# A fused retention and gated-convolution kernel: 128x128 products turn keys and queries one double chunk ahead, the tensor engine's phase is cut in four, and keys arrive in float32

## The chip, the cores and the metric

The kernel runs on one core of a Trainium2 chip. The core has a tensor engine (PE in the profile, with PEld for its weight loads), a vector engine (DVE), a scalar engine (ACT), GpSimd (POOL) and a sync engine (SP) that here only issues transfers; 16 DMA engines move data between HBM and the on-chip memory SBUF. Matmul results land in a second memory, PSUM, in banks. The metric is the device time of one execution in microseconds; the median of three runs is given. The profile describes one execution, whose "span" is the time from its first to its last instruction.

## What is computed

Eight batches, eight heads, 576 tokens, head width 64. First a retention layer (attention with an exponential decay in place of the softmax), then a gated unit whose gate is a causal convolution over five tokens:

```python
scores = scale * np.matmul(q, k.transpose(0, 1, 3, 2))
gamma = 1.0 - 2.0 ** (-5.0 - np.arange(H))
Dmat = np.where(rel >= 0, gamma[:, None, None] ** rel[None], 0.0)   # rel = query position - key position
x = np.matmul(scores * Dmat, v)                 # then heads side by side: B x S x 512
gate_pre[:, t] = sum over k of conv_w[k] * x[:, t - 4 + k]           # 5 taps, zeros before the start
out = (sigmoid(gate_pre) * (x @ w_val)) @ w_out
```

All inputs and the output are float32: q, k and v are 9.4 MB each and so is the output, and the two weight matrices are 1 MB each.

## The kernel before

**Tiling.** 256 tokens of one batch (all eight heads) make a "double chunk". There are 18, numbered m: two for each of the eight batches, and after each group of four batches one "tail" that gathers the last 64 tokens of those four. Within a double chunk, token 2p+r sits on partition p, so that two tokens follow one another in a row; `ab` is the half of the partitions (the first or second 128 tokens), `pr` a pair of heads, `i` the head within it, `r` the token within its row. The decay is split into a factor by key token (`gin`, multiplied into the values) and one by query token (`gout`, multiplied into the result), so that in between only a 0/1 mask is needed.

**Steps for one double chunk m.** (1) Load q, k, v. (2) Cast to bfloat16: `cast_q`, and `cast_v` that also multiplies by `gin`, mostly on GpSimd. Keys, except the first ones, are loaded by `load_keys` (line 100): a DMA issued by GpSimd that casts on its way. (3) "Turn" keys and queries, so that the head width lies on the partitions: products with an identity matrix on the tensor engine into the PSUM bank `tps`, and a copy from there into `kq`. (4) `scores` (64x64 products of turned keys and queries), `masks` on the vector engine. (5) `update`: the state of the batch, keys times values, accumulated in the PSUM bank `st` and copied by `take_state` on the scalar engine. (6) `values` and `carried`: masked scores times values, plus state times queries, into the banks `o0` and `o1`; `take_x` (line 343) multiplies by `gout` on the vector engine and writes the result into the tile `xg`. (7) One double chunk later, `conv(m-1)`: 40 products of 64x64 with diagonal matrices, over shifted columns of `xg`, into two banks of the pool `psg`, and `gate` (a sigmoid on the scalar engine). (8) `value(m-1, i)`: eight products of 128x128 with `wvb`, and on the vector engine z = gate times value. (9) Two later, `project(m-2, i)`: four products of 128x128 with `wob`, copied by the scalar engine (line 433) and stored.

**Quarters and whole array.** Products with 64 rows and 64 columns use a quarter of the array, and four of them on different quarters run beside one another ("64*64" in the profile); `value` and `project` use the whole ("128*128").

**Order.** It is written out by hand: every engine takes its instructions in the order of the program. The tiling framework sets the waits between engines, by semaphores, from the tiles that instructions share. Start-up (lines 471 to 576) treats the first double chunks one by one, turns double chunks 1 to 4, and leaves the loop with two turned ahead. In the loop from line 578 one pass does, on the tensor engine: carried, scores, turning of half of m+2 mixed with `update(m, 1)`, convolution, values, carried, turning of the other half mixed with `update(m+1, 0)`, the end of the convolution, `scores(m+1, 0)` (all quarters), and then value, project, value, project (whole array). Turning a double chunk takes 64 products of 64x64 (line 268): 2 for keys and queries, 2 halves, 4 pairs, 2 tokens, 2 heads. `take_turned` (line 278) copies one half of keys and queries at once.

**Transfers.** Loads of q and v and the stores are issued by SP, in the program's order; q and v have five buffers (`LB = 5`), the bfloat16 keys seven.

Of the kernel before, what the change touches and what calls it, by code (L numbers as in the profile page):

```python
# [21 lines left out]
def kernel(  # L22
# [10 lines left out]
    nc = tc.nc  # L33
# [12 lines left out]
    LB = 5  # L46
# [33 lines left out]
    with tc.manual_schedule():  # L80
# [14 lines left out]
        def load(name, m):  # L95
            t = ld.tile([P, H, R, D], F32, name=f"f{name}", bufs=1 if name == "k" else LB)
            fetch(nc.sync, t, {"q": q, "k": k, "v": v}[name], m)
            loaded[name, m] = t

        def load_keys(m):  # L100

            kb = bfp.tile([P, H, R, D], BF16, name="kb", bufs=7)
            fetch(nc.gpsimd, kb, k, m)
            kbf[m] = kb

        cwn = consts.tile([KC * NP, P], F32, name="cwn")
        nc.scalar.dma_start(out=cwn, in_=moe_conv_w.rearrange("k (o i) -> (k o) i", i=P))
        load("k", 0)
        load("q", 0)
        load("v", 0)  # L110
        load("q", 1)
        load("v", 1)
# [9 lines left out]
        load_wv(nc.sync, 0)  # L122
        for m in range(2, LB + 1):
            load("q", m)
            load("v", m)
# [19 lines left out]
        load_keys(1)  # L145
# [44 lines left out]
        for pr in range(NP):  # L190
            nc.scalar.activation(gout[:, pr, :], posi, AF.Exp, bias=lsc, scale=lcol[:, pr:pr + 1])

        warm = consts.tile([P, 1], F32, name="warm")
        nc.scalar.activation(warm, lsc, AF.Sigmoid)
# [7 lines left out]
        tbank = ps_t.tile([P, 2, NP, R, HP], BF16, name="tps")  # L202
        whole = lambda t: t.rearrange("p a o r n -> p (a o r n)").bitcast(F32)
# [4 lines left out]
        def prep_conv_weights():  # L208
            cps = whole(tbank)[:, 0:KC * NP]
            nc.tensor.transpose(cps, cwn, identf[0:KC * NP, 0:KC * NP])  # L210
            cps = cps.rearrange("p (k o) -> p k o", k=KC)
            nc.vector.tensor_copy(cw[:, :, 0::2], cps[:, :, 0::2])
            for i in range(2):
                nc.vector.tensor_copy(cw[half[1 - i], :, 1::2], cps[half[i], :, 1::2])
# [11 lines left out]
        def cast(dst, src, copies):  # L226

            h = 0
            for (copy, n) in copies:
                copy(dst[:, h:h + n], src[:, h:h + n])  # L230
                h += n
            assert h == H

        def cast_k(m, *copies):
            kbf[m] = bfp.tile([P, H, R, D], BF16, name="kb", bufs=7)
            cast(kbf[m], loaded["k", m], copies)

        def cast_q(m, *copies):
            qbf[m] = bfp.tile([P, H, R, D], BF16, name="qb")
            cast(qbf[m], loaded["q", m], copies or ((nc.gpsimd.tensor_copy, H),))  # L240

        def cast_v(m, *engs):
            vbf[m] = bfp.tile([P, H, R, D], BF16, name="vb")
# [19 lines left out]
        def turns(which, m, ab, bank=None):  # L263

            src = (kbf, qbf)[which][m]
            dst = tbank[:, which] if bank is None else bank
            rows = half[ab]
            return [[(lambda pr=pr, r=r, i=i: nc.tensor.transpose(  # L268
                dst[half[i], pr, r, :], src[rows, 2 * pr + i, r, :], idb[rows, :]))
                for r in range(R) for i in range(2)] for pr in range(NP)]  # L270

        def turned_tile(m):
            if m not in kq:
                kq[m] = tp_sb.tile([P, 2, NP, 2, R, HP], BF16, name="kq")
            return kq[m]

        def take_turned(m, ab):
            nc.scalar.copy(turned_tile(m)[:, :, :, ab], tbank)  # L278
# [7 lines left out]
        def scores(m, r):  # L286
# [3 lines left out]
            return [[mm(s[i][half[ab], pr, 0:n], lhsT=kq[m][half[i], 0, pr, ab, r, :],  # L290
                        rhs=kq[m][half[i], 1, pr, ab, cols(m, r), :].rearrange("p r n -> p (r n)"),
# [32 lines left out]
        def carried(m, turn):  # L324
# [4 lines left out]
            for g in range(2):  # L329
                group = []  # L330
                for r in range(R) if kind == "tail" else (0,):
                    for i in range(2):
# [4 lines left out]
                        for pr in (2 * g, 2 * g + 1):  # L337
                            group.append(add(m, ab, pr, i, cols(m, r), lhsT=before[key][half[i], pr, :],
                                             rhs=kq[m][half[i], 1, pr, ab, cols(m, r), :].rearrange("p r n -> p (r n)")))
# [17 lines left out]
        def update(m, ab):  # L357
# [5 lines left out]
            return [[mm(st[b][half[i], pr, :], lhsT=kbf[m][half[ab], 2 * pr + i, r, :],  # L363
# [24 lines left out]
        def conv(n):  # L388

            g = [ps_g.tile([P, 2, 2 * P], F32, name="g") for _ in range(2)]  # L390
# [16 lines left out]

        def spare(pool, name):
            return pool.tile([P, DM], F32, name=name)
# [35 lines left out]
        def keep_warm(n):  # L445

            for _ in range(n):
                nc.tensor.matmul(whole(tbank), zeros[:, 0:P], zeros, start=True, stop=True)

        def turn_early(which, m, copies):  # L450

            banks = [ps_g.tile([P, NP, R, HP], BF16, name="g") for _ in range(2)]
            run(*[turns(which, m, ab, banks[ab]) for ab in range(2)])
            dst = turned_tile(m)[:, which]
            for ab in range(2):
                copies[ab](dst[:, :, ab], banks[ab])

        def turn_both(which, m, copies):

            src = (kbf, qbf)[which][m]  # L460
            bank = tbank.rearrange("p a o r n -> p (a o r n)").rearrange("p (o r n) -> p o r n", o=NP, r=R)
            for pr in range(NP):
                for r in range(R):
                    for i in range(2):
                        nc.tensor.transpose(bank[half[i], pr, r, :], src[:, 2 * pr + i, r, :], ident)  # L465
            dst = turned_tile(m)[:, which]
            for ab in range(2):
                copies[ab](dst[:, :, ab], bank[:, :, :, half[ab]])
# [3 lines left out]
        cast_k(0, (v_copy, 4), (s_copy, 4))  # L472
        turn_early(0, 0, (v_copy, s_copy))
        prep_conv_weights()
        keep_warm(5)
        cast_q(0, (v_copy, 4), (s_copy, 4))
        turn_early(1, 0, (v_copy, s_copy))
        load_wv(nc.scalar, 1)
        run(scores(0, 0))
        masks(0, 0, 0)  # L480
        masks(0, 0, 1)
        cast_v(0, (nc.gpsimd, 6), (nc.vector, 2))
        load_keys(2)
        keep_warm(8)


        turn_early(0, 1, (s_copy, v_copy))
        run(update(0, 0))
        take_state(0, 0)
        keep_warm(3)  # L490
        cast_q(1, (s_copy, 8))
        run(carried(0, 1))
        run(scores(0, 1))
        masks(0, 1, 0)
        masks(0, 1, 1)
        run(update(0, 1))
        take_state(0, 1)
        turn_early(1, 1, (s_copy, s_copy))
        cast_v(1)
        load("q", 6)  # L500
        load("v", 6)
        load_keys(3)
        load_wo()
        keep_warm(3)
        run(*values(0, 1))
        run(*values(0, 0))
        run(carried(0, 0))
        take_x(0, 0)
        take_x(0, 1)
        run(scores(1, 0))  # L510
        for o in range(NP):
            prep_diagonals(o, nc.vector)
        masks(1, 0, 0)
        masks(1, 0, 1)
        keep_warm(3)
        run(update(1, 0))
        take_state(1, 0)

        def early(m):

            hi, lo = conv(m - 1)
            run(carried(m, 1))
            run(scores(m, 1))
            masks(m, 1, 0)
            masks(m, 1, 1)
            run(lo, hi)
            gate(m - 1, 0)
            gate(m - 1, 1)
            run(update(m, 1))
            take_state(m, 1)  # L530
# [5 lines left out]

        early(1)
        cast_q(2, (s_copy, 4), (v_copy, 4))
        prep_wv(s_copy, 0)
        prep_wv(v_copy, 1)  # L540
        cast_v(2)
        load("q", 7)
        load("v", 7)
        load_keys(4)
        cast_q(3)
        cast_v(3)
        load("q", 8)
        load("v", 8)
        load_keys(5)
        turn_both(0, 2, (s_copy, v_copy))  # L550
        value(0, 0)
        turn_both(1, 2, (s_copy, v_copy))
        run(update(2, 0))
        take_state(2, 0)
        value(0, 1)
        run(scores(2, 0))
        masks(2, 0, 0)
        masks(2, 0, 1)
        early(2)
        cast_q(4)  # L560
        cast_v(4)
        load_keys(6)
        cast_q(5)
        turn_both(0, 3, (s_copy, v_copy))
        value(1, 0)
        turn_both(1, 3, (s_copy, v_copy))
        project(0, 0)
        run(scores(3, 0))
        run(update(3, 0))
        take_state(3, 0)  # L570
        value(1, 1)
        masks(3, 0, 0)
        masks(3, 0, 1)
        turn_both(0, 4, (s_copy, v_copy))
        project(0, 1)
        turn_both(1, 4, (s_copy, v_copy))

        for m in range(3, ND + 1):
            now, unit, last = ok(m), ok(m - 1), m == ND
            ahead = ok(m + 2)  # L580
            if ok(m + LB + 1):
                load("q", m + LB + 1)
                load("v", m + LB + 1)
            if ok(m + 4):
                load_keys(m + 4)
# [85 lines left out]
```

## Time and profile before

| | |
|---|---|
| median of 3 runs | 200.89 us (194.89 to 204.69) |
| profiled execution | 198.55 us, its span 196.8 us |
| granted tensor clock, mean | 0.91 of full speed |
| DVE, ACT, POOL busy | 104.9, 91.1, 72.3 us |
| instructions of the tensor engine | 4159 matmuls, as many weight loads |

The busy time of an engine is an average over parts with different limits, so the parts have to be read apart. Three of the costliest groups on the engines beside the tensor engine, one line each: operation, output and inputs, shapes and count, then busy time and mean length, then the idle time of that engine before it and what ended it.

```profile
L298 DVE TENSOR_TENSOR p<-s,mask 128x512 bf16<-128x512 f32 x64 | 41.1, 685 | 10.3 <-PE s L259 10.3
L278 ACT COPY kq<-tps 128x1024 bf16<-128x1024 bf16 x26 | 26.4, 1017 | 0.3 <-PE tps L268 0.2
L230 POOL CAST qb<-fq 128x1024 bf16<-128x1024 f32 x15 | 15.5, 1031 | 2.8 <-PE o L312 1.5
```

A mask takes 685 ns on the vector engine and four of them are needed for a double chunk; copying half of a turned double chunk takes 1017 ns on the scalar engine; casting the queries of a double chunk takes 1031 ns on GpSimd.

### The profile page before, as it was taken

What the parts mean: (1) busy time and instruction counts of PE and PEld (TensorE: products, weight loads), DVE (VectorE), ACT (ScalarE), POOL (GpSimd) and SP (SyncE); (2) the same over time, 40 slices, a digit from 0 to 9 for tenths busy, and PEclk for the clock granted to TensorE, in tenths of its full rate; (3) what the DMA queues carried; (4) which work ended last, traced back from release to release, by engine and by line L of the source; (5) the groups of instructions that cost most, each with busy time, mean ns of one, the idle gap of its engine ahead of it and who ended that gap; (6) DMA issues with size and microseconds to landing.
All of it is one profiled execution on the core that took longest, in us unless ns stands there. A gap on an engine that the chain in (4) does not pass through costs nothing.

```text
span 196.8 us, 9108 instructions
## 1 busy us (share of the span) xinstructions
PE 156.4 (79%) x4159; PEld 110.5 (56%) x4159; DVE 104.9 (53%) x201; ACT 91.1 (46%) x155; POOL 72.3 (37%) x72
## 2 busy tenths in 40 slices
PE   6068959979769695969799872989499989979990
PEld 2023538666556573737587652566368758656640
DVE  5224384675727364735557642366457766756130
ACT  2841605324455554635475541355727648423330
POOL 6068525838152707160734707038505120000000
PEclk9755885599999999978999997599999999999998
DMA  5999999999999897987799997559911202202223
GB/s 161 294 275 285 246 242 269 266 279 245 197 285 203 240 186 210 176 211 152 220 210 253 260 227 186 53 137 169 184 58 60 110 25 90 107 6 110 107 102 111
DMA packets 69060, 35.46 MB, mean 180 GB/s; under 512 B 29578, under 2 KB 63902, under 8 KB 69022
## 3 DMA queue, kind: packets, MB, share of 16 engines
q1 hardware_dynamic: 48144, 29.10, 51.7%
q0 software_dynamic: 20400, 4.98, 26.5%
q8 instruction: 32, 0.52, 1.1%
q10 hardware_dynamic: 478, 0.80, 1.1%
q14 instruction: 6, 0.05, 0.1%
HBM read 30.42 MB, written 9.44 MB: 202 GB/s over the span
## 4 chain that ended last, share of the span: by engine, by line
PE 66%; issue 9%; DVE 9%; SPq 5%; DMA 5%; ACT 4%; ACTq 1%; DVEq 0%
PE g L415 18%; PE g L425 16%; PE g L259 11%; PE o L312 7%; DVE xg L347 5%; DMA fv<-in_v_dram 5%; PE tps L268 5%; PE s L259 4%; SPq L87 4%; PE st L259 2%; DVE p L298 2%; SPq L120 1%; PE tps L465 1%; PE s L415 1%; DVE dg L217 1%
## 5 line engine op out<-in xcount | busy, mean ns | idle before, releaser
L247 POOL TENSOR_TENSOR vb<-fv,gin 128x1024 bf16<-128x1024 f32 (+1 forms) x18 | 34.0, 1887 | 82.9 <-issue 58.9
L298 DVE TENSOR_TENSOR p<-s,mask 128x512 bf16<-128x512 f32 x64 | 41.1, 685 | 10.3 <-PE s L259 10.3
L418 DVE TENSOR_TENSOR z<-gate,g 128x512 bf16<-128x512 f32 x34 | 23.4, 688 | 35.5 <-PE g L415 35.2
L415 PE MATMUL g<-xg,wvb 128*128 128x256 bf16 x272 | 38.3, 287 | 0.6 <-ACT wvb L223 0.5
L433 ACT COPY ob<-g 128x512 f32<-128x512 f32 x34 | 20.0, 587 | 40.2 <-PE g L425 40.2
L425 PE MATMUL g<-wob,z 128*128 128x512 bf16 x144 | 38.3, 393 | 0.0
L259 PE MATMUL g<-xg,dg 64*64 64x256 bf16 x720 | 31.4, 280 | 6.2 <-DVE xg L347 5.6
L415 PEld LDWEIGHTS <-wvb 128*128 128x128 bf16 x288 | 27.8, 102 | 12.3 <-issue 4.9
L347 DVE TENSOR_TENSOR xg<-o,gout 128x512 bf16<-128x512 f32 x32 | 22.2, 744 | 17.1 <-PE o L312 17.1
L405 ACT ACTIVATE gate<-g 128x512 f32<-128x512 f32 x36 | 21.4, 604 | 20.8 <-PE g L259 20.7
L259 PEld LDWEIGHTS <-dg 64*64 64x64 bf16 x720 | 23.0, 110 | 7.8 <-issue 7.7
L278 ACT COPY kq<-tps 128x1024 bf16<-128x1024 bf16 x26 | 26.4, 1017 | 0.3 <-PE tps L268 0.2
L259 PE MATMUL s<-kq 64*64 64x128 bf16 (+1 forms) x576 | 17.4, 222 | 7.0 <-issue 3.4
L259 PE MATMUL st<-vb,kb 64*64 64x64 bf16 x512 | 15.5, 200 | 8.5 <-issue 8.4
L425 PEld LDWEIGHTS <-z 128*128 128x128 bf16 x144 | 14.3, 101 | 11.1 <-issue 1.3
L259 PEld LDWEIGHTS <-kq 64*64 64x64 bf16 x576 | 12.7, 111 | 8.9 <-issue 8.6
L259 PEld LDWEIGHTS <-kb 64*64 64x64 bf16 x512 | 12.2, 113 | 9.7 <-issue 9.7
L230 POOL CAST qb<-fq 128x1024 bf16<-128x1024 f32 x15 | 15.5, 1031 | 2.8 <-PE o L312 1.5
L375 ACT CAST sd<-st 128x256 bf16<-128x256 f32 x24 | 9.0, 375 | 16.2 <-PE st L259 16.2
L268 PEld LDWEIGHTS <-kb 64*64 64x64 bf16 x480 | 10.7, 113 | 8.3 <-ACT kb L230 4.6
L312 PE MATMUL o<-p,vb 64*64 64x128 bf16 (+1 forms) x576 | 13.5, 220 | 0.9 <-issue 0.9
L87 POOL DMA_DIRECT2D kb<-in_k_dram x15 | 14.1, 943 | 0.1
(75 smaller groups left out, 143.3 us busy)
## 6 DMA issues: line engine op xcount, KB each, us to landing
fq<-in_q_dram SPq DMA_DIRECT2D x16, 512.0 KB, 7.7
fv<-in_v_dram SPq DMA_DIRECT2D x16, 512.0 KB, 7.9
out_dram<-ob SPq DMA_DIRECT2D x32, 256.0 KB, 3.2
kb<-in_k_dram POOLq DMA_DIRECT2D x15, 256.0 KB, 6.3
fq<-in_q_dram SPq DMA_DIRECT2D x8, 128.0 KB, 4.4
fv<-in_v_dram SPq DMA_DIRECT2D x8, 128.0 KB, 4.7
out_dram<-ob SPq DMA_DIRECT2D x6, 128.0 KB, 2.3
fk<-in_k_dram SPq DMA_DIRECT2D x1, 512.0 KB, 4.0
```

The source lines that it names most:

```text
L87: eng.dma_start(out=t.rearrange("p h r d -> p h (r d)"), in_=src[b, :, c * W:(c + 1) * W, :].rearrange("h (p r) d -> p h (r d)", r=R))
L247: eng.tensor_tensor(vbf[m][:, h:h + n], loaded["v", m][:, h:h + n], g[:, h:h + n].unsqueeze(3).to_broadcast([P, n, R, D]), op=ALU.mult)
L259: return lambda: nc.tensor.matmul(*a, skip_group_check=True, **kw)
L268: return [[(lambda pr=pr, r=r, i=i: nc.tensor.transpose(dst[half[i], pr, r, :], src[rows, 2 * pr + i, r, :], idb[rows, :])) for r in range ...
L278: nc.scalar.copy(turned_tile(m)[:, :, :, ab], tbank)
L298: nc.vector.tensor_tensor(p[:, :, 0:n], sps[m, r][i][:, :, 0:n], mask[dcs[m][0], r].unsqueeze(1).to_broadcast([P, NP, n]), op=ALU.mult)
L312: nc.tensor.matmul(o, start=key not in opened, stop=False, skip_group_check=True, **kw)
L347: nc.vector.tensor_tensor(xg[b // GB][:, b % GB, :, PAD + t0:PAD + t0 + P].rearrange("p o (n r) -> p o r n", r=R), ops[m, ab], gout[:, :, ...
L405: nc.scalar.activation(t, gps[n][i], AF.Sigmoid)
L415: nc.tensor.matmul(vps[:, j, :], lhsT=wvb[:, o, 2 * i + j, :], rhs=xs(n, slice(0, P), o, PAD), start=(j == 0 and o == 0), stop=(j == 1 and ...
L418: nc.vector.tensor_tensor(z, gsb[n][i], vps, op=ALU.mult)
L425: nc.tensor.matmul(o, lhsT=zsb[n, j // 2][:, j % 2, i * P:(i + 1) * P], rhs=wob[:, j, :], start=(j == 0), stop=(j == NP - 1))
```

## The change

It does four things. Keys are loaded in float32 by SP like queries and values (`load` for k, q and v alike, four buffers each), and cast by GpSimd (`cast_k`); `load_keys` is gone. Turning uses the whole array: two heads side by side form a 128x128 block, so a double chunk takes 16 products of 128x128 in place of 64 of 64x64; keys and queries go through the bank one after the other, each with its own copy; this happens one double chunk ahead instead of two. The bfloat16 keys and queries lie in another order for this (`[P, NP, R, 2, D]`), and `kq` keeps 128 columns together. The pass through the loop is cut into four parts: quarters (scores, carried, update, convolution, update of the next, scores), whole array (turn the keys, value, project), quarters (values, carried), whole array (turn the queries, value, project). And the start-up is no longer written out chunk by chunk: the loop begins at m = 0, with `soon` marking the first two passes; the first keys are cast and copied on the vector engine, and the table `gout` is computed in two parts, the second in the first pass.

The purpose is to spend fewer instructions on turning, to relieve GpSimd of issuing transfers, and to mix quarters with whole-array products.

```diff
-    LB = 5
+    LB = 4
         def load(name, m):
-            t = ld.tile([P, H, R, D], F32, name=f"f{name}", bufs=1 if name == "k" else LB)
+            t = ld.tile([P, H, R, D], F32, name=f"f{name}")
-        def load_keys(m):
-            kb = bfp.tile([P, H, R, D], BF16, name="kb", bufs=7)
-            fetch(nc.gpsimd, kb, k, m)
...
-        def turns(which, m, ab, bank=None):
-            return [[(lambda pr=pr, r=r, i=i: nc.tensor.transpose(
-                dst[half[i], pr, r, :], src[rows, 2 * pr + i, r, :], idb[rows, :]))
-                for r in range(R) for i in range(2)] for pr in range(NP)]
+        def turn(which, m, bank=None):
+            for pr in range(NP):
+                for r in range(R):
+                    nc.tensor.transpose(dst[:, pr, r, :], src[:, pr, r, :, :].rearrange("p i d -> p (i d)"), ident)
-        def take_turned(m, ab):
-            nc.scalar.copy(turned_tile(m)[:, :, :, ab], tbank)
+        def take_turned(which, m, bank, *copies):
+                kq[m] = tp_sb.tile([P, 2, NP, R, P], BF16, name="kq", bufs=2)
+            for (copy, n) in copies or ((nc.scalar.copy, NP),):
+                copy(kq[m][:, which, o:o + n], bank[:, o:o + n])
...
+        for m in range(ND + 1):
+            if now:
+                run(scores(m, 0))
+                masks(m, 0, 0)
+                masks(m, 0, 1)
...
+                run(carried(m, 1))
+                run(pairs(update(m, 1)), lo[0:2])
+                take_state(m, 1)
...
+            run(lo[2:10], hi[0:8])
+            if unit:
+                gate(m - 1, 1)
+            if soon:
+                run(hi[8:10])
+            else:
+                run(pairs(update(m + 1, 0)), hi[8:10])
+                take_state(m + 1, 0)
+            if unit:
+                gate(m - 1, 0)
+            if now:
+                run(scores(m, 1))
...
+            if nxt:
+                bank = turn(0, m + 1)
+                take_turned(0, m + 1, bank)
+            if m > 1:
+                value(m - 1, 1)
+                project(m - 2, 0)
+            if ok(m + 2):
+                for (name, f) in (("k", cast_k), ("q", cast_q), ("v", cast_v)):
+                    f(m + 2)
+                    if ok(m + 2 + LB):
+                        load(name, m + 2 + LB)
...
             run(*values(m, 1))
             run(*values(m, 0))
             run(carried(m, 0))
             take_x(m, 0)
             take_x(m, 1)
...
+            if nxt:
+                bank = turn(1, m + 1)
+                take_turned(1, m + 1, bank)
+            if m == 0:
+                prep_gout(1)
+                nc.scalar.activation(warm, lsc, AF.Sigmoid)
+                load_wo()
             if unit:
                 value(m - 1, 0)
             if ok(m - 2):
...
                 project(m - 2, 1)
+            if soon:
+                run(update(m + 1, 0))
+                take_state(m + 1, 0)
```

## The prediction

> **What bounds the kernel now.** I read the page first (slices, queues, chain by engine), then the chain of waits in order of time, then single stretches and the start of the timeline.
>
> ```profile
> span 196.8 us, 9108 instructions
> ...
> PEclk9755885599999999978999997599999999999998
> DMA  5999999999999897987799997559911202202223
> ...
> q1 hardware_dynamic: 48144, 29.10, 51.7%
> q0 software_dynamic: 20400, 4.98, 26.5%
> q8 instruction: 32, 0.52, 1.1%
> ...
> PE 66%; issue 9%; DVE 9%; SPq 5%; DMA 5%; ACT 4%; ACTq 1%; DVEq 0%
> ```
>
> The tensor engine holds 66% of the chain, but 9% (17 us) is "issue", time in which it waited for nothing visible. DMA is full for two thirds of the run and idle afterwards. The clock row shows half speed in the slices from 15 to 40 us. In order of time:
>
> ```profile
> 62.32 0.22 PE s L259 x14
> 63.09 0.91 PE g L259 x32
> 64.00 0.67 PE o L312 x36
> 64.80 1.59 issue
> 66.97 0.24 PE s L259 x16
> 67.21 0.98 PE g L415 x8
> ...
> 73.98 2.06 issue
> ...
> 118.05 3.70 issue
> ...
> 156.73 1.36 DVE xg L347 x2
> ```
>
> One pass of the loop runs from 62.0 to 70.9 us: quarters, a hole, quarters, whole array. The holes recur in the same part of each pass. Two stretches, one in a hole and one late in the run (columns: length, then busy time and count for PE, PEld, DVE, ACT, POOL, then clock, DMA share, GB/s):
>
> ```profile
> 73.80:76.10 2.30, 0.24 (x28) 0.13 (x19) 1.30 (x2) 0.10 (x1) 2.30 (x2) 1.00 0.99 289
> ...
> 160.00:170.00 10.00, 10.00 (x275) 7.19 (x275) 7.68 (x12) 5.65 (x11) 0.00 (x0) 1.00 0.22 83
> ```
>
> In the hole the tensor engine stands still while DMA is at 0.99; late, with DMA at 0.22, it is never idle. Counted in order, the instruction after a hole is number 2241, 2753, 3265, 4545, 4801, 5057, 5569 or 6081 of the tensor engine: all lie a multiple of 256 apart. Queue q8 moved 0.52 MB in 32 packets, so 16 KB each, 64 bytes times 256. The holes are waits for the engine's own instructions; with the one at 55 us they add up to 14.3 us. From the entry into one block to the first instruction of the next takes 4.0 us (62.39 to 66.39), 4.3 (71.76 to 76.04), three times 5.3 to 6.5 (the longest from 109.36 to 115.83). A stretch of quarters eats 256 instructions in about 2.7 us, and waits for the rest.
>
> The second item is the start:
>
> ```profile
> 5.61 3.13 ACT L191 ACTIVATE gout<-posi,lsc,lcol 128x576 f32<-128x576 int32 x4
> ...
> 10.82 0.43 PE L268 MATMUL g<-idb,kb 64*64 64x64 bf16 x16 [4.45 <-ACT kb L230]
> ...
> 15.60 0.86 PE L259 MATMUL s<-kq 64*64 64x128 bf16 x16 [0.51 <-DVE kq L456]
> ```
>
> The first scores run at 15.6 us, because half of the first key cast stood behind `gout` and a table load on the scalar engine. The loop at m = 3 begins at 52 us.
>
> **What the Trainium skill says.** "Runtime: NRT & Kernel Launch", section "Instruction fetch mechanics": instructions stream in blocks of 16 KiB, 256 of them, over the sequencer's own DMA queue while the current block runs, a cost "mostly hidden". The block size agrees; hidden it is not here, 14.3 us. "DMA: Bandwidth & Descriptors", section "Queues, rings and completion order": a DMA engine takes turns between the queues it has work for, packet by packet. That fits the lateness of blocks under load. "TensorEngine Tiling (Array Packing)", section "Key Properties": changing the tiling mode drains the engine. The trace agrees in kind: the first `value` product starts 0.15 us after the last score, where scores start some 10 ns apart, and the first quarter 0.31 after the last projection, against 0.216 between projections; 0.23 us a round trip. For the missing price of a 128-column product, "TensorE: Matmul & The Clock Gate", section "Back-to-back issue gap", gives 56 ns alone and about 81 in a stream with weight loads.
>
> **The change, part by part: one full pass of the loop.** From passes without holes: 154.05 to 162.42 us is 8.4 (second chunk of its batch, with a wait for `xg`), 162.42 to 169.59 is 7.2; mean 7.8. Over the whole loop it was worse: from 52.0 to 184.2 us minus two tails of 6.8 and 6.3 leaves 119 for 13 full passes, 9.2 each.
> - Removed: 64 quarter products for turning. Sixteen of them with sixteen of the update start between 62.38 and 62.65, 8.4 ns each: 64 x 8.4 = -0.55 us.
> - Added: 16 products of 128x128. No row of before has them. The nearest, line 465, does 16 of 128 rows by 64 columns in 0.64 us, two side by side: 80 ns per full width. With the page's 56 to 81 ns the bounds are 0.9 and 1.3; I take 1.3, as each has a weight load of its own. The low end would make a pass 0.4 shorter.
> - Added: a second round trip between modes, +0.23.
> - Moved: `conv(m-1)` now lies wholly ahead of `take_x(m)`, so its last products no longer wait for the vector engine (1.05 us in every other pass). `value(m-1, 0)` still carries such a wait, after its first product, again when both chunks are of one batch. The two `take_x` need 1.4 us and the queries' turning hides 0.65: 0.75 left, so -0.15 on average.
> - Holes: a pass falls from about 240 products to 192, 384 instructions, 1.5 blocks instead of 1.9, and no stretch eats 256 of them in under 4.1 us (112 quarter products in 2.2 us, then 16 whole-array ones in 1.9). Against 4.0 to 4.3 us, mostly nothing is left; for 5.3 to 6.5 some is. I take 0.2 a pass.
>
> Sum: 7.8 - 0.55 + 1.3 + 0.23 - 0.15 + 0.2 = 8.8, against 9.2.
>
> Beside the path: the scalar engine does two copies of 1.02, two state copies of 0.375, two gates of 0.60 and two output copies of 0.59, 5.2 us in 8.8; each copy of turned data waits for a product and is due a whole-array part (2.4 us) or more later. Vector engine: 4 x 0.685 + 2 x 0.744 + 2 x 0.688 = 5.6. GpSimd loses 0.94 for issuing and gains 1.03 for the key cast: 4.0, two passes ahead of need. On SP a load stands behind an output store that waits for the scalar engine, and carries data for six passes ahead, so nobody feels it. DMA: q0's 20400 packets took 26.5% x 196.8 x 16, 41 ns each, q1's 34 ns. 19456 key packets move from 41 to 34 ns: from 154 us of all engines to about 145. Four-deep buffers see the same order of load, below the end of the compute.
>
> **The start.** Key cast whole on the vector engine: 5.6 + 0.75; turning and copy to 8.1; queries (cast 0.6, behind four warming products) turned by 10.6, copied by 11.2; first scores 11.3 instead of 15.6. Then masks, state, second scores, values at the half clock: `take_x(0)` at 17.6. Queries of m = 1 are copied by 19.3. Behind that copy on the scalar engine are the second part of `gout` (4 x 0.53) and a table load (1.28), and behind these the state copy that `carried(1, 1)` waits for: 23.4, a new wait of about 4 us. Convolution to 26, gates and `wvb` on the scalar engine to 28.6, values, `value(0, 0)`: m = 2 begins at 34 to 35, m = 3 at 43 to 44. Before it was 52, with 1 to 1.5 us of work ahead.
>
> **Total.** 35 + 14 passes x 8.8 + tails 7.6 and 6.6 + last convolution and projections as before (184.2 to 196.8, 12.6) = 185.0 us of span. The profiled execution was 1.75 us above its span: 187; the cheaper price of the 128-column products would take off 14 x 0.4 = 6. I set 185.
>
> **The rivals.**
> A. The holes stay, since DMA is as full as now and a block late by 5 us is still late: 0.8 more per pass, 14 x 0.8 = 11: 196. For it: 5.3 to 6.5 us was seen three times, and float32 keys add bytes (512 against 256 in a packet). Against: fewer packets and longer blocks.
> B. Nothing gained or slower: the whole-array turning, the second mode round trip and the wait at `value(m-1, 0)` cost 1.5 to 2 us a pass and eat the holes, and the scalar engine's start-up chain (gout, table, gates, wvb) takes all the gain at the start: 35 + 9 + 14 x 9.6 + 14 + 12.6 = 204. For it: late passes of before already run at 7.8 with nothing to remove. Against: only the high end of every price gives it.
> C. Cheap 128-column products (56 ns) and no holes at all: 35 + 14 x 8.2 + 13.5 + 12.6 + 1.75 = 178, or 173 with a start 5 us better and full clock from 20 us on.
>
> **Numbers.** Forecast 0.5, A 0.15, B 0.18, C 0.17. Range 172 to 200: C's end and A are in, B's upper half is out. Faster by over 2% (below 196.9): forecast, C and over half of A, 0.77; within 2%: 0.11; slower: 0.12.
>
> **What would show it.** Right: "issue" in the chain falls under 6 us; a pass takes 8.5 to 9; eight 128x128 turning products take 0.5 to 0.65 us; first scores near 11 us; a wait of some 4 us at m = 1 for `sd`; `value` waits about 0.75 us for `xg` in every other pass; DMA busy until about 140 us. Wrong: holes over 1 us at block edges, the scalar engine ending the tensor engine's waits inside the loop, POOL casts waiting for key loads, or m = 2 later than 40 us.

## The result, and the profile after

| | before | after |
|---|---|---|
| median | 199.16 us (4 runs, 194.89 to 204.69) | 181.31 us (4 runs, 180.43 to 182.71) |
| span of the profiled execution | 196.8 us | 179.1 us |
| loop reaches m = 4 | 62.0 us | 54.8 us |
| from there to the last convolution | 122.2 us | 111.8 us |
| rest | 12.6 us | 12.4 us |

The change makes the kernel faster: the ratio after to before is 0.925, 95% interval 0.910 to 0.940. Ratios, here and below, take only the undisturbed runs of both kernels (of the kernel before, only two beside the first four variants), so they need not equal the ratios of the medians. Of the 17.7 us by which the profiled span is shorter, the start gave 7.2 and the loop 10.3. A pass of the loop begins at another step in the two kernels, so this boundary is not quite the same work in both.

The prediction read half clock only at the start of the kernel before. Its clock row has two stretches more, in the loop: 3.4 us from 86.2 us and 6.8 us from 120.3, behind the hole at 83.6 and in that at 118.05. They cost time too. Three passes of before, one at full clock and the two with half clock (start and end, length, busy time and count of PE, PEld, DVE, ACT, POOL, then clock, DMA share, GB/s):

```profile
62.02:70.86 8.84, 7.25 (x233) 5.46 (x232) 5.22 (x9) 4.84 (x8) 3.77 (x3) 1.00 1.01 222
80.39:90.97 10.58, 8.83 (x234) 6.10 (x233) 5.26 (x8) 4.74 (x8) 3.76 (x3) 0.84 0.85 199
114.13:128.62 14.49, 9.74 (x241) 6.85 (x240) 5.23 (x9) 4.84 (x8) 3.76 (x3) 0.76 0.75 149
```

With its holes left out, a pass at half clock keeps the tensor engine busy for 8.83 or 9.74 us instead of 7.25, some 4 us for the two together. The changed kernel has no half clock in the loop. So the loop's gain is that of the holes and of about 4 us of clock; passes without either are no shorter than before (7.93 us on average now, 7.77 before). Part of the start's gain may be clock too: ahead of m = 4 the kernel before ran 24 us at half clock, the changed one 14.

The page of the changed kernel, the lines that answer to those shown of before (span, clock and DMA by slice, queues, chain by engine):

```profile
span 179.1 us, 7593 instructions
...
PEclk9999558699999999999999999999999999999998
DMA  4999999999897799999999697876842111111334
...
q1 hardware_dynamic: 68256, 38.54, 73.2%
q0 software_dynamic: 576, 0.52, 1.8%
q8 instruction: 26, 0.43, 1.0%
...
PE 74%; DVE 13%; ACT 4%; issue 4%; DMA 2%; ACTq 0%; DVEq 0%
```

"issue" fell from 9% to 4% of the chain. The tensor engine's instructions came in 26 blocks instead of 32 (q8). DMA is still full for more than half of the run. All keys now travel on q1: 68256 packets took 73.2% x 179.1 x 16, 31 ns each.

The chain of waits in order of time, most of one pass of the loop and then the longest hole (start, length, what):

```profile
64.53 0.55 PE tps L264 x8
65.08 0.87 PE g L408 x8
...
66.22 0.59 PE g L418 x2
66.82 0.74 PE o L308 x39
67.56 1.36 DVE xg L343 x2
...
68.96 0.92 PE g L408 x7
...
91.98 0.89 issue
```

Eight turning products take 0.55 us where the stretch before ends in quarters; from one to the next it is 56 ns. Ahead of the last `value` products stands the vector engine's `xg`, 1.36 us for two halves, of which turning the queries hides one part. The longest hole is 0.89 us, where it was 3.70. There are five, 0.35 to 0.89 us, together 3.1, again a multiple of 256 instructions apart.

Two passes of the loop, the first without the wait for `xg`, the second with it (start and end, length, busy time and count of PE, PEld, DVE, ACT, POOL, then clock, DMA share, GB/s):

```profile
54.84:62.28 7.44, 7.33 (x184) 5.60 (x186) 5.36 (x8) 4.93 (x8) 2.87 (x4) 1.00 0.79 205
62.28:70.68 8.40, 7.50 (x192) 5.70 (x193) 5.33 (x8) 4.82 (x8) 5.04 (x4) 1.00 1.08 332
```

Full passes cost 7.44 or 8.40 us, with holes 8.17 on average. Between the two kinds lies 0.96 us, all of it in the stretch with the wait (0.80 us idle).

The timeline of the start (start, length, what; in brackets the wait ahead and who ended it):

```profile
10.75 0.31 PE L254 MATMUL s<-kq 64*64 64x128 bf16 x8 [0.67 <-ACT kq L272]
...
23.54 0.43 PE L308 MATMUL o<-kq,sd 64*64 64x128 bf16 x8 [3.30 <-ACT sd L371]
...
27.98 1.08 POOL L226 CAST qb<-fq 128x1024 bf16<-128x1024 f32 x1
28.12 3.31 DVE L217 CAST wvb<-wvf 128x512 bf16<-128x512 f32 x2
28.98 2.16 POOL L242 TENSOR_TENSOR vb<-fv,gin 128x1024 bf16<-128x1024 f32 x1
31.49 1.89 PE L408 MATMUL g<-xg,wvb 128*128 128x256 bf16 x8 [4.53 <-DVE wvb L217]
```

First scores come at 10.75 us instead of 15.60, followed by two waits that were 0.5 us at most before: 3.30 us for `sd` and 4.53 us for the converted value weights.

### The profile page after: what moved, and what is told of

Same layout as the page of the kernel before. It is cut to its first block, busy times and chain, and to the rows that moved or that the text cites. A ratio compares the mean times of both kernels' runs of the same rounds, so it can differ in the third digit from the quotient of the medians.

```text
span 179.1 us, 7593 instructions
## 1 busy us (share of the span) xinstructions
PE 148.3 (83%) x3344; PEld 108.8 (61%) x3377; DVE 105.9 (59%) x191; ACT 93.4 (52%) x154; POOL 74.0 (41%) x69
## 3 DMA queue, kind: packets, MB, share of 16 engines
q1 hardware_dynamic: 68256, 38.54, 73.2%
## 4 chain that ended last, share of the span: by engine, by line
PE 74%; DVE 13%; ACT 4%; issue 4%; DMA 2%; ACTq 0%; DVEq 0%
PE g L408 18%; PE g L418 16%; PE g L254 13%; PE tps L264 9%; PE o L308 8%; DVE xg L343 6%; PE s L254 6%; PE st L254 3%; DMA fk<-in_k_dram 2%; DVE wvb L217 2%; DVE p L294 2%; DVE dg L211 2%; ACT gout L187 1%; PE s L408 1%; PE tps L442 1%
## 5 line engine op out<-in xcount | busy, mean ns | idle before, releaser
L272 ACT COPY kq<-tps 128x1024 bf16<-128x1024 bf16 x34 | 34.6, 1019 | 23.0 <-PE tps L264 22.8
L226 POOL CAST qb<-fq 128x1024 bf16<-128x1024 f32 (+1 forms) x18 | 18.3, 1019 | 49.9 <-issue 21.7
L418 PE MATMUL g<-wob,z 128*128 128x512 bf16 x111 | 34.7, 379 | 2.1 <-issue 0.4
L242 POOL TENSOR_TENSOR vb<-fv,gin 128x1024 bf16<-128x1024 f32 x18 | 34.5, 1916 | 3.6 <-DMA fv<-in_v_dram 3.5
L411 DVE TENSOR_TENSOR z<-gate,g 128x512 bf16<-128x512 f32 x34 | 23.4, 687 | 17.6 <-PE g L408 17.6
L226 POOL CAST kb<-fk 128x1024 bf16<-128x1024 f32 x17 | 17.8, 1050 | 8.8 <-DMA fk<-in_k_dram 6.7
L254 PEld LDWEIGHTS <-kq 64*64 64x64 bf16 x576 | 12.6, 109 | 9.6 <-issue 9.6
L254 PE MATMUL st<-vb,kb 64*64 64x64 bf16 x512 | 13.9, 196 | 0.0
L308 PEld LDWEIGHTS <-vb 64*64 64x64 bf16 x576 | 8.6, 107 | 8.8 <-issue 8.7
L308 PE MATMUL o<-kq,sd 64*64 64x128 bf16 x192 | 9.4, 222 | 4.7 <-ACT sd L371 4.0
L254 PEld LDWEIGHTS <-kb 64*64 64x64 bf16 x512 | 12.4, 112 | 0.8 <-issue 0.8
L308 PE MATMUL o<-p,vb 64*64 64x128 bf16 (+1 forms) x576 | 11.4, 216 | 1.6 <-DVE p L294 1.6
```

Of the source, the lines that this page charges most:

```text
L226: copy(t[:, o:o + n], src[:, o:o + n])
L242: eng.tensor_tensor(vbf[m][:, h:h + n], loaded["v", m][:, h:h + n], g[:, h:h + n].unsqueeze(3).to_broadcast([P, n, R, D]), op=ALU.mult)
L254: return lambda: nc.tensor.matmul(*a, skip_group_check=True, **kw)
L272: copy(kq[m][:, which, o:o + n], bank[:, o:o + n])
L308: nc.tensor.matmul(o, start=key not in opened, stop=False, skip_group_check=True, **kw)
L411: nc.vector.tensor_tensor(z, gsb[n][i], vps, op=ALU.mult)
```

## The experiments

Five theories stand behind most of the expectations, which also use letters of their own (rival B of one of them is not the prediction's B). **F:** the holes are waits for instruction blocks, and these are late because DMA is full. **N:** the number of tensor instructions alone decides over the holes. **D:** the holes are other waits. **K:** keys on the software queue (GpSimd's casting DMA) were what cost. **S:** only the start changed. Times are medians of four runs, six for the last kernel; all ratios are to the kernel before, run beside each variant on the same chip. The changed kernel was not run beside its variants, so differences of a few us from its 181.31 are weaker than the ratios, and are checked by stages in the traces.

### The kernel before without its later loads

```diff
         def load(name, m):
+            if m > LB:
+                loaded[name, m] = loaded[name, 1 + (m - 1) % LB]
+                return
         def load_keys(m):
+            if m > 6:
+                kbf[m] = kbf[m % 7]
+                return
```

> The kernel before, but from m = 6 (queries, values) and m = 7 (keys) on no input is loaded: the tiles of earlier double chunks are used again, so the later results are those of other inputs. Everything else, the tensor engine's instructions above all, is as before. Theory F (the holes in the loop are waits of the tensor engine for blocks of its own instructions, which come late because DMA is full): from some 55 us on DMA carries only outputs, the holes at multiples of 256 shrink from 14.3 us to under 3, a full pass falls from 9.2 to about 7.8 us, and the time to 185 to 190 us. Rival D (the holes are waits for another engine or for data of the loop): holes stay at the same places, 195 us or more. Rival K (the holes come from the software queue that carries the keys) also expects a fall here and is told apart by the next two runs.

Measured: 187.0 us (185.0 to 191.5), ratio 0.956 (0.936 to 0.975). Its page (DMA by slice; chain by engine):

```profile
DMA  5999999990020112120311311223031211311223
...
PE 73%; DVE 13%; issue 5%; ACT 5%; POOL 1%; ACTq 0%; DVEq 0%; POOLq 0%
```

"issue" falls from 9% to 5%, and the waits at block edges from 14.3 to 6.1 us, at the same places; D falls. So full DMA makes the blocks late, as F says, for 8.2 us. But eight waits of 0.25 to 1.2 us stay while DMA is nearly idle. They end 3.2 to 4.2 us after the engine entered the block before: with the old mix of instructions it can outrun its fetch even then. F with "under 3 us" is not the whole of it. No half clock is left in the loop.

### The keys alone: float32 keys in the kernel before

```diff
-            t = ld.tile([P, H, R, D], F32, name=f"f{name}", bufs=1 if name == "k" else LB)
+            t = ld.tile([P, H, R, D], F32, name=f"f{name}", bufs=LB + 1 if name == "k" else LB)
...
             if ok(m + LB + 1):
+                load("k", m + LB + 1)
...
-            if ok(m + 4):
-                load_keys(m + 4)
...
+                    cast_k(m + 3, (g_copy, H))
```

> The kernel before with the third part of the change alone: keys loaded in float32 by SP and cast on GpSimd, nothing issued by GpSimd but w_out. Theory F: as many instructions, DMA as full, so the holes stay: 10 to 15 us of them, time within 3% of before, 194 to 204 us. Rival K (keys on the software queue hold up DMA and GpSimd): holes mostly gone, 182 to 188 us.

Measured: 196.71 us (196.34 to 197.12), ratio 1.015 (1.006 to 1.024), no gain. The holes stay: "issue" is 9% of the chain, one hole 3.58 us long. From m = 4 to the last convolution it takes 122.1 us, as before. K falls. Its start-up, that of before but for the keys, reaches m = 4 at 59.8 us with 3.4 us at half clock, where the kernel before took 62.0 with 24: some 2 of the 7.2 us that the start gained may thus be the clock's.

### Keys and whole-array turning, without the four parts

The loop of before, with keys as above, where the mixed-in quarter products of the turning are replaced by 16 whole-array ones next to `value` and `project`, still two double chunks ahead.

```diff
-                run(turn(0, 0), pairs(update(m, 1)))
+                run(pairs(update(m, 1)))
...
+            if ahead:
+                turn_whole(0, m + 2)
...
+            if ahead:
+                turn_whole(1, m + 2)
```

> The run with float32 keys, and in the loop also the turning by 16 products of 128x128, two double chunks ahead, placed in the whole-array part; a pass keeps its two parts, quarters and then whole array, and the start-up is that of before. 192 products a pass as in the changed kernel, but 152 quarter products (304 instructions) in one stretch of some 3.5 us. Theory F in its full form (number and spreading both count): a block edge inside most stretches, holes about half of before, 0.4 to 0.8 us a pass, time 188 to 194 us. Rival N (the number of instructions alone counts): passes as in the changed kernel, 8.2 us, holes under 4 us in all, time 184 to 187 us. Rival S (all the gain is in the start-up): 196 us or more.

Measured: 187.54 us (186.38 to 188.56), ratio 0.967 (0.955 to 0.980). From m = 4 to the last convolution 113.1 us. Its page:

```profile
q8 instruction: 27, 0.44, 1.0%
...
PE 74%; DVE 16%; ACT 5%; issue 2%; ACTq 0%; POOL 0%; DVEq 0%; POOLq 0%
```

No wait at a block edge is left, though quarters still run in one stretch and DMA is full until some 115 us. From m = 4 until then no block of 256 instructions lasts under 4.2 us. So the four parts are not needed against the holes; fewer instructions are enough. S falls too, since the start-up is that of before. Its full passes take 8.36 us on average (two successive ones 16.72), those of the changed kernel without holes 7.93 (two take 15.85, from 119.77 to 135.62): the four parts are worth 0.43 us a pass, about half of it a shorter wait for `xg` in every other pass (1.2 to 1.4 us here, 0.8 there).

### The changed kernel with keys on the software queue again

```diff
-            t = ld.tile([P, H, R, D], F32, name=f"f{name}")
...
+            if name == "k" and m:
+                t = ld.tile([P, H, R, D], BF16, name="kd")
+                fetch(nc.gpsimd, t, k, m)
+                loaded[name, m] = t
+                return
+            t = ld.tile([P, H, R, D], F32, name=f"f{name}", bufs=1 if name == "k" else LB)
```

> The changed kernel with keys again loaded by a casting DMA of GpSimd (from m = 1 on), into bfloat16 in the order of memory; GpSimd then only reorders them, in place of the cast. Theory F: the tensor engine's program is the same, holes stay small, 180 to 185 us, at most 2% above the changed kernel's 181.3. Rival K: the gain is lost, 190 us or more.

Measured: 181.15 us (180.97 to 181.46), ratio 0.935 (0.927 to 0.943); the changed kernel has 181.31 and 0.925. From both sides, then, the way the keys come brings no gain that can be measured here. Its profiled execution has five holes again, 4.6 us, the longest 1.76 with 3.4 us at half clock behind it, so kernels with the same products differ this much in their holes.

### The changed kernel with more instructions and no more work

```diff
-                    nc.tensor.matmul(vps[:, j, :], lhsT=wvb[:, o, 2 * i + j, :], rhs=xs(n, slice(0, P), o, PAD), ...)
+                    rhs = xs(n, slice(0, P), o, PAD)
+                    if dcs[n][0] == "full":
+                        for e in range(2):
+                            nc.tensor.matmul(vps[:, j, e * P:(e + 1) * P], lhsT=wvb[:, o, 2 * i + j, :],
+                                             rhs=rhs[:, e * P:(e + 1) * P], ...)
...
-                nc.tensor.matmul(o, lhsT=zsb[n, j // 2][:, j % 2, i * P:(i + 1) * P], rhs=wob[:, j, :], ...)
+                for e in range(NP):
+                    nc.tensor.matmul(o[:, e * P:(e + 1) * P], lhsT=zsb[n, j // 2][:, j % 2, i * P:(i + 1) * P],
+                                     rhs=wob[:, j, e * P:(e + 1) * P], ...)
```

> The changed kernel with 40 more products of the tensor engine in a full pass and no more work: each value product of 256 columns is cut into two of 128, each output product of 512 columns into four of 128 (192 products a pass become 232; before the change there were 240). The columns are the same, so at 56 ns for 128 columns, 109 for 256 and about 216 for 512 this alone adds some 0.1 us a pass, 1.5 us. Theory N (waits for blocks of instructions grow with their number, whatever they are): the waits of the tensor engine at every 256th product come back, 8 to 11 of them, 8 to 13 us instead of 3.1, and the kernel takes 188 to 194 us. Rival B (what ran the engine short of instructions before was the dense run of 64 short quarter products, not the number over a pass): waits stay at 2 to 5 us and the time at 181 to 184.

Measured: 186.14 us (183.54 to 187.68), ratio 0.939 (0.926 to 0.951); the changed kernel has 181.31 and 0.925. Its page, and below it two lines of its chain of waits:

```profile
DMA  5999999999947799999599629795781121111324
...
q8 instruction: 32, 0.52, 1.2%
...
PE 77%; DVE 8%; issue 6%; ACT 4%; DMA 2%; ACTq 0%; DVEq 0%
```

```profile
50.82 2.82 issue
...
102.11 1.75 issue
```

The holes are back: eight instead of five, 10.3 us instead of 3.1, each again at a multiple of 256 instructions from the others (numbers 961, 1473, 2241, 2497, 3265, 3777, 4033, 5057 of the tensor engine). All lie ahead of 125 us, while DMA is full; afterwards the same passes run without one. This kernel has the four parts, the whole-array turning and the float32 keys; only the number of instructions is near that of before (232 products a pass; 240 before, 192 in the changed kernel). So it is the number that decides while DMA is full, as N says, and a dense run of quarters (rival B of this expectation) isn't needed.

The time stays below the 188 that N gave as its low end, and the intervals of the two ratios overlap. Only the traces show where the added waits went. Until m = 4 the profiled execution takes 4.0 us more than the changed kernel, with holes of 1.25 and 2.82 us there. From m = 4 to the last convolution it takes 2.7 us more: 3.7 us more of holes and 3.4 us at half clock, against passes that are themselves shorter, which the expectation lacked. Two late ones take 15.55 us (128.22 to 143.77), where the changed kernel needs 15.85, since the half-width `value` products no longer wait for `xg`:

```profile
133.54 1.39 DVE L343 TENSOR_TENSOR xg<-o,gout 128x512 bf16<-128x512 f32 x2 [0.82 <-PE o L308]
...
133.89 1.06 PE L411 MATMUL g<-xg,wvb 128*128 128x128 bf16 x16
```

They run while the vector engine still writes `xg`. So the wait for `xg` was not one for data: these products read the double chunk before, and the vector engine writes the next one into other columns of the same tile. The dependence that the framework sets vanishes when each product reads 128 columns instead of 256; why the wider read is held to overlap was not looked into.

### The changed kernel without its later loads

```diff
         def load(name, m):
+            if m > LB + 1:
+                loaded[name, m] = loaded[name, 2 + (m - 2) % LB]
+                return
```

> The changed kernel without the loads of keys, queries and values from double chunk 7 on: later double chunks take the tiles that earlier ones loaded (the work on them stays). Theory N: there is little left to gain from the transfers, at most the 3.1 us of remaining waits for instructions, 177.5 to 181.5 us. Rival L (the passes after the change are still paced by the input transfers): passes get shorter by more than 0.3 us each, below 176.

Measured: 178.25 us (177.29 to 178.62), ratio 0.906 (0.899 to 0.913): 3.1 us less than the changed kernel (0.925), and none of its holes left. In the kernel before a like edit was worth 4.4% by the ratio, here 2.1%. The passes otherwise stay as long as they were (7.44 and 8.41), and no block of 256 instructions lasts under 4.2 us: the input loads don't pace them.

### Value weights converted earlier

```diff
                 masks(m, 0, 0)
                 masks(m, 0, 1)
+            if m == 1:
+                prep_wv(v_copy, 1)
             if m == 0:
                 keep_warm(4)
...
             if m == 1:
-                prep_wv(v_copy, 1)
                 prep_wv(s_copy, 0)
```

> The changed kernel, with VectorE's conversion of the first half of the value weights (two instructions of 1.65 us) ahead of the work of pass 1 that waits for the second part of the output gate, instead of behind it. If the wait of 4.5 us for that conversion at 27 to 31.5 us is only one of order on VectorE: about 3 us less, 176 to 179.5. If the table itself arrives late, or the value products then wait for something else of the start (the copies of the second half, the first x): 179.5 to 182.

The edit puts the two instructions between the first masks of pass 1 and its convolution. Measured: 175.56 us (173.75 to 177.84), ratio 0.890 (0.881 to 0.900): 5.8 us less than the changed kernel, more than the 3 expected. In the timeline of its start:

```profile
21.37 1.04 POOL L226 CAST qb<-fq 128x1024 bf16<-128x1024 f32 x1 [0.34 <-DMA fq<-in_q_dram]
21.52 1.50 DVE L217 CAST wvb<-wvf 128x512 bf16<-128x512 f32 x2
...
26.88 1.03 PE L408 MATMUL g<-xg,wvb 128*128 128x256 bf16 x8 [0.18 <-ACT gate L401]
```

The value products begin at 26.88 us instead of 31.49, and take 1.03 us instead of 1.89, since they run at full clock, which is back at 26.2 us here; in the changed kernel they fall into a second stretch of half clock, 30.8 to 34.3 us, behind the long wait. m = 2 begins 5.9 us earlier. That is all of the gain; late passes are unchanged (15.84 us for two).

### Output products ahead of the waiting value products

```diff
-            if unit:
+            late = ok(m - 2) and dcs[m][2] > 0
+            if unit and not late:
                 value(m - 1, 0)
             if ok(m - 2):
                 project(m - 2, 1)
+            if late:
+                value(m - 1, 0)
```

> The changed kernel, with the second output products of a pass (project of two chunks ago) ahead of its last value products in the passes in which these wait for VectorE's xg (7 waits, 0.6 to 0.8 us each, 5.4 us in all). If the wait is only one of order: 3.5 to 5.5 us less, 176 to 178. If VectorE's later end moves the wait elsewhere (the next masks stand behind the z product that the value products feed): 179 to 182.

Measured: 175.47 us (171.92 to 177.27), ratio 0.880 (0.868 to 0.893): 5.8 us less than the changed kernel by the medians, more by the ratio (0.925 there). Its chain of waits in one such pass:

```profile
122.65 0.55 PE tps L264 x8
123.21 0.86 PE g L418 x4
124.07 1.00 PE g L408 x8
...
125.16 0.70 DVE z L411
```

`xg` is gone from the chain; the 0.86 us of output products stand where the wait was. Two late passes take 15.27 us instead of 15.85, over seven pairs 4.1 us; the wait was one of order. The span of its profiled execution is 175.1 us, 4.1 less than that of the changed kernel, 3.0 of it from m = 4 to the last convolution, where six such pairs lie, and the rest in the start. What the ratio shows beyond that stays open. Something new shows, too: `z` of the vector engine now stands in the chain at the start of the next pass.

### Both

The two diffs above, together.

> The changed kernel with both edits at once: the conversion of the value weights ahead of the work that waits for the output gate, and the second output products ahead of the last value products wherever these wait for xg. Alone they brought 5.8 us each (181.3 to 175.6 and 175.5). If the two waits are independent and their sizes add, some 8 to 11 us less than the changed kernel: 170 to 173.5 us. If part of each single gain was the state of the run's start or of the waits for instructions rather than the edit: 173.5 to 176.

Measured: 171.89 us (171.19 to 174.23, six runs), where the changed kernel has 181.31 (180.43 to 182.71) and the kernel before, run beside it, 198.98 (192.26 to 206.44). The gain of 9.4 us falls within the 8 to 11 expected. By stages of the profiled executions the edits are nearly independent: m = 4 comes 5.2 us earlier than in the changed kernel (6.3 with the earlier conversion alone, where half clock at the start lasted 3.4 us less), and from there to the last convolution it takes 4.1 us less (3.0 with the other order alone). It beats both kernels. Its page:

```profile
span 170.2 us, 7626 instructions
...
PE 78%; DVE 10%; ACT 4%; issue 2%; DMA 2%; ACTq 0%; DVEq 0%
```

## Why the prediction was right, and where its terms were off

The forecast was 185.0 us, the time is 181.31, on the side of rival C. The mechanism held; that the total came this near is in part luck, since the passes came out 8.8 us shorter than forecast and the start and the tails 3.2 us longer, and since the sum gave 187 before it was set to 185. The sizes, step by step:

- **Holes are waits for instruction blocks, and the change nearly ends them.** Right, and shown: by their places 256 apart, by fewer holes with fewer instructions, by their return when products are cut up, and by their end when loads are left out. Forecast 0.2 us a pass, measured 3.1 us in all, 0.22 for each of 14 full passes (one of the holes, 0.89, lies in a tail). "Fewer instructions" holds: it makes blocks last longer. The four parts, which were to keep any stretch from eating a block too fast, weren't needed for that: two-part passes with whole-array turning had no holes either. And load is not the only cause: 6.1 us stayed in the kernel before without later loads. That holes are followed by half clock, and so cost more than their length, was not in the prediction. Rival A (holes stay, since DMA stays full) fell, since a full DMA costs only where blocks are asked for too fast.
- **Added turning products, the term most out of size.** Taken at some 81 ns, 1.3 us a pass; they start 56 ns apart, 0.9 us. This alone is 0.4 us a pass, 5.6 in all. "TensorE: Matmul & The Clock Gate" of the Trainium skill, section "Back-to-back issue gap", gives both figures; here the figure for a product alone was the measured one, although each product had its own weights and they came in a stream; the 81 was not seen.
- **Removed quarters and second mode round trip.** Forecast -0.55 + 0.23 = -0.32. In a pass without waits the quarters, with the change to whole array behind them, took 3.44 us before (162.42 to 165.86) and take 2.87 now (2.18 from 128.18 and 0.69 from 132.65), though they now contain two such changes of 0.15 us. So the removed quarters were worth 0.72. The extra round trip cost what was forecast: both changes, 0.15 and 0.31 us, occur twice a pass now. A gain that was not forecast hides it: before, the second `value` started 0.36 us after the last product of the first `project`, where 0.22 is the pace, and that step is gone.
- **The wait for `xg`.** Forecast 0.75 us in every other pass, measured 0.80. That it wasn't a wait for data and could be taken away was not foreseen.
- **A pass.** Forecast 8.8; measured 8.17. The cheaper turning, 0.4, the quarters, 0.17, and the step that is gone, 0.15, make up 0.7, near the 0.63.
- **The start.** First scores forecast at 11.3, measured 10.75; wait for `sd` until 23.4, measured until 23.54. Then m = 2 was to begin at 34 to 35 and begins at 37.3: the prediction put the gates and `wvb` on the scalar engine, done by 28.6, and missed the half of `wvb` on the vector engine, done at 31.43. The experiment with the earlier conversion shows that this wait, with the slower products behind it, is worth 5.9 us, 4.9 in the kernel with both edits.
- **Total.** 37.3 + 14 x 8.17 + tails of 8.3 and 6.8 + 12.4 = 179.2, the span; the 8.17 is worked out from this sum, so it proves nothing by itself. Against the forecast the passes gave 8.8 us, and the start took 2.3 and the tails 0.9.
- **DMA.** Forecast 145 us of all engines for q0 and q1, busy until about 140. Now 75.0% x 179.1 = 134 us, busy until about 130. Packets of q1 took 31 ns instead of the 34 assumed. That DMA isn't the bound held: without later loads only the holes vanished.
- **Rival B** needed the high end of every price, and the turning came at the low end. Its wait at `value` exists, but it takes the place of a longer one: passes with and without a wait for `xg` differ by 0.96 us now, and differed by 1.20 before (8.37 and 7.17). Its sum, too, comes to 205, not 204.
- **Signs.** Two of those named for "right" did not come: "issue" is 3.8% of the chain, 6.8 us and not under 6 (3.1 of it at block edges), and a pass is shorter than 8.5. One of those named for "wrong" did: key casts on GpSimd waited for key loads, 3.9 us at the start and 0.8 to 1.1 us three times later. No wait of the tensor engine ends with a cast on GpSimd.

## What to carry to other kernels

When the tensor engine stands still for no visible reason, number its instructions: gaps a multiple of 256 apart were here waits for its own instructions, most of them in stretches with full DMA, and then fewer, larger products are worth more than their busy time. After such a change, read the chain again, since what remains may be order alone: here output products moved ahead of waiting ones, and two conversions moved ahead of other work of their engine, gave half as much again as the change itself. A start-up sum must follow every queue that feeds the first products, not only the longest.

## What the runs showed of the hardware that was not expected

- The conversion of 128x512 float32 weights on the vector engine took 0.41 us each in the kernel before, and 1.27 and 2.12 in the changed one. In the timeline above each ends 0.3 us after a GpSimd instruction does: the first runs from 28.12 to 29.39 and GpSimd's cast ends at 29.05; the second until 31.43, and GpSimd's product ends at 31.14. With the earlier conversion the first took 1.16 us (GpSimd's cast ends at 22.41, it at 22.68), and the second, in a pause of GpSimd, 0.41. "SBUF — State Buffer" of the Trainium skill, section "Who interferes with whom", says that a vector engine cast in a two-port mode and a GpSimd instruction lock each other out of a shared pair of ports, and the later one waits for the whole of the other. The times agree with that; that this cast runs in such a mode no run shows, and none was made for it alone.
- Waits for instructions exist without load: up to 1.2 us each in the kernel before without its later loads, with DMA at 0.24 of its time or less around them. They end 3.2 to 4.2 us after the entry into the block before. In the changed kernel under load the five waits end 5.2 to 5.9 us after it.
- A pass with 232 products had holes up to 2.82 us, 10.3 in all; with 192 and the same loads the changed kernel had 3.1 in all: a fifth more instructions tripled the waiting. Its variants with 192 had single holes up to 1.76 us.
- In the loop the granted clock fell to half for 3.4 us (once 6.8), and each of these seven stretches, in four kernels, began 2.1 to 4.6 us after the start of a hole of 1.75 us or more. Two holes of this size, 1.78 and 2.06 us, had none behind them, and no shorter hole had one. That the hole brings it on was not tried.
